# One attention-and-MLP kernel: the first block's second MLP product by quarters of w_ch2, and the scaling of w_ch2 mostly on GpSimd

## The chip, the cores and the metric

One core of a Trainium2 chip. The metric is the device time of one execution in microseconds (us). Engines are named as the profile names them: PE is TensorE's matmuls and PEld its weight loads, DVE is VectorE, ACT is ScalarE, POOL is GpSimd, SP is SyncE, whose queue issues most DMAs. A "q" behind an engine is its sequencer.

## The reference

A pooled attention over 8 batches of 8 heads, 576 rows and head size 64, followed by a residual MLP mixer on 512 channels:

```python
k_p = k.reshape(B, H, Sp, pool, D).mean(axis=3)        # pool = 8, Sp = 72
v_p = v.reshape(B, H, Sp, pool, D).mean(axis=3)
scores = scale * np.matmul(q, k_p.transpose(0, 1, 3, 2))
attn = softmax(scores)
x = np.matmul(attn, v_p)                               # then (B, S, H*D) = (8, 576, 512)

a1 = alpha1 * x + beta1
tok = np.einsum('ts,bsd->btd', w_tok, a1)
u = x + lam * tok
a2 = alpha2 * u + beta2
ch = np.maximum(a2 @ w_ch1, 0.0) @ w_ch2               # 512 -> 2048 -> 512
return u + lam * ch
```

## The kernel before, in words

**Blocks and chunks.** The 8 x 576 rows are cut into 36 chunks of 128 rows, and four chunks make a block; nine blocks (`n` = 0 to 8) go through the MLP one after the other. While block `n` is in the MLP, batch `n + 1` goes through attention, so that PE always has matmuls of one or the other.

**The MLP of a block.** `mlp_A(n, j)` makes one of 16 slices of the hidden layer: four matmuls into a PSUM tile `ps_h` (L662), then a ReLU on ACT into `H4` (L669). `mlp_B(n, m, part)` (L674) is the second product for chunk `m` and one quarter `part` of w_ch2: four matmuls (L682) that add to the chunk's PSUM tile. Behind the last quarter DVE adds the result to the chunk `u_sb` (L689), and `store` issues the output on SP's queue (L698). This plain form is used in blocks 0 and 1 only (`FIRST = 2`). From block 2 on, the second product is a 2 x 2 Strassen-like scheme (`product`, L748) on sums of quarters of w_ch2, which DVE makes once, late in block 1 (`weight_sum`, L712).

**lam.** In block 0 w_ch2 is as loaded, and DVE multiplies the product by `lam_bc` in PSUM (L688) before it adds it (L689). From block 1 on, w_ch2 itself has been multiplied by lam: `scale_w2(g, i)` (L709) does one of the four pieces of quarter `g`, 128 x 512 in bf16, in place (L710). There are 16 pieces. A piece can be scaled only when block 0 has used it for the last time, and must be done before block 1 uses it.

**The order of the work** is written out by hand. In each block a list `todo` of (position, step) is sorted by position, and the steps are issued in that order; every engine then runs its own instructions strictly in that order and waits on semaphores for the others. Position 16 is where the second product of a block starts.

**Attention of the next batch, as far as it is touched.** `load_q_bf` loads q through GpSimd's queue (L79); SP transposes it into `qT` (L397). `sum_k` (L185, L187) sums pairs of k rows on GpSimd, `att_K` makes the pooled k on PE (`ps_kp`, L445 and L451), and DVE copies it to `kp` (L457). `att_V` sums pairs of v rows on DVE in three halvings (L483: 72 x 1024, 72 x 512, 72 x 256). `att_S4` makes the scores from `qT` and `kp` (`ps_s`, L513; `ps_r`, L520), ACT takes the exponentials (L542), and `att_AV` multiplies by v (`ps_av`, L556, L560); DVE normalizes (L562, L564) and scales (`xs`, L578, L571). `mix_T` mixes the tokens (`ps_tok`, L614), DVE adds x (L618), ACT casts (L622), and `mix_uT` has SP transpose the result into `u_fm` for the next block's `mlp_A` (L633).

**PSUM.** Two buffers of tag `ch` hold the products of chunks 0 and 1; six buffers of tag `gp` serve all else, the products of chunks 2 and 3 (`ps_ch2`) included. A new tile waits until the engine that reads the old one is done.

Of the kernel before, what the change touches and what calls it, by code (L numbers as in the profile page):

```python
# [11 lines left out]
ALU = mybir.AluOpType  # L12
# [11 lines left out]
def kernel(  # L24
# [18 lines left out]
    nc = tc.nc  # L43
# [23 lines left out]
    def new_batch(b):  # L67
        st1[b] = {"qT": [None] * 2, "ET": [None] * H, "raw": [None] * 2, "q": [None] * 2,
                  "k": [None] * 2, "v": [None] * 2}
# [130 lines left out]
    lam_bc = const.tile([P, DM], FP, tag="lam_bc", name="lam_bc")  # L200
# [66 lines left out]
    for i in range(2):  # L267
# [11 lines left out]
                            in1=pool_v[0:32, 1:16:2], op=ALU.add)  # L279
# [74 lines left out]
    w2 = [const.tile([P, 4, DM], BF, tag=f"w2_{g}", name=f"w2_{g}") for g in range(4)]  # L354
# [8 lines left out]
    def scale_w1(i, cc):  # L363
        nc.scalar.activation(out=w1[i][:, cc, :], in_=w1[i][:, cc, :], func=AF.Copy, bias=0.0,
                             scale=al2_cols[:, cc:cc + 1])
# [285 lines left out]
    def mlp_A(n, j, t0=0, t1=512):  # L651

        if t0 == 0:
            ps_A[j] = gp("ps_h")
        ps_h = ps_A[j]
        one = t1 < 512
        for cc in range(4):
            if n == 0:
                rhs = u_fm[0][:, cc, 0, 0:257] if one else u_fm[0][:, cc, t0 // 256:2, 0:256]
            else:  # L660
                rhs = u_fm[n][:, cc, :]
            nc.tensor.matmul(out=ps_h[:, t0:t1 + one], lhsT=w1_of(cc, j), rhs=rhs,  # L662
                             start=(cc == 0), stop=(cc == 3))
        if one:
            nc.vector.tensor_copy(out=bias_cols[:, j:j + 1], in_=ps_h[:, 256:257])
            return
        if (n, j // 4) not in H4:
            H4[n, j // 4] = work.tile([P, 4, 512], BF, tag="H4", bufs=4, name="H4")
        nc.scalar.activation(out=H4[n, j // 4][:, j % 4, :], in_=ps_h, func=AF.Relu,  # L669
                             bias=bias_cols[:, j:j + 1], scale=1.0)  # L670
# [3 lines left out]
    def mlp_B(n, m, part):  # L674
        if part == 0:
            if m < 2:
                ps_ch[m] = psB.tile([P, DM], FP, tag="ch", bufs=2, name="ps_ch")
            else:
                ps_ch[m] = gp("ps_ch2")
        ps = ps_ch[m]  # L680
        for j in range(4 * part, 4 * part + 4):
            nc.tensor.matmul(out=ps, lhsT=H_of(n, j)[:, 128 * m:128 * m + 128], rhs=w2[j // 4][:, j % 4, :],  # L682
                             start=(j == 0), stop=(j == NJ - 1))
        if part == 3:
            b, c = chunks[4 * n + m]
            u = st2[b, c]["u"]
            if n == 0:
                nc.vector.tensor_tensor(out=ps, in0=lam_bc, in1=ps, op=ALU.mult)  # L688
            nc.vector.tensor_tensor(out=u, in0=u, in1=ps, op=ALU.add)  # L689
            store(n, m)  # L690
# [15 lines left out]
    HALF = DM // 2  # L706
    wino = {}

    def scale_w2(g, i):  # L709
        nc.vector.tensor_tensor(out=w2[g][:, i], in0=w2[g][:, i], in1=lam_bc, op=ALU.mult)  # L710

    def weight_sum(i, g):  # L712
        lo, hi = w2[g], w2[g + 2]
# [20 lines left out]
    def hidden_sum(n, i, g):  # L734

        lo, hi, S2, S3 = H4[n, g], H4[n, g + 2], wino["S2"][g], wino["S3"][g]
        top, low = slice(0, HALF), slice(HALF, DM)
        o, a, b, op = {
            3: (S3, lo[:, :, top], lo[:, :, low], ALU.subtract),
            1: (lo[:, :, low], lo[:, :, low], hi[:, :, low], ALU.add),  # L740
            2: (S2, lo[:, :, low], lo[:, :, top], ALU.subtract),
            4: (lo[:, :, top], hi[:, :, top], S2, ALU.subtract),
        }[i]
        nc.vector.tensor_tensor(out=o, in0=a, in1=b, op=op)  # L744
# [189 lines left out]
    for n in range(NBLK):  # L934
        todo = []
        for j in range(0 if n else 4, NJ):
            if n == 0 and j < 8:
                todo.append((j, lambda j=j: mlp_A(0, j, 0, 256)))
                todo.append((j + (1.01 if j < 7 else 0.3), lambda j=j: mlp_A(0, j, 256, 512)))
            else:  # L940
                at = 8 * (j // 4 % 2) + 4 * (j // 8) + j % 4 if n >= FIRST else j
                todo.append((at, lambda j=j: mlp_A(n, j)))
        for m in range(4 if n < FIRST else 0):
            for part in range(4):
                at = 16 + 2 * part + (m if m < 2 else 6 + m)
                todo.append((at, lambda m=m, part=part: mlp_B(n, m, part)))
        if n == 0:
            for i in range(3):
                for cc in range(4):
                    todo.append((17.0 + 2.0 * i + 0.5 * cc, lambda i=i, cc=cc: scale_w1(i, cc)))  # L950
            for piece in range(8):
                at = 27.3 + 0.55 * piece
                todo.append((at, lambda k=piece: scale_w2(k // 4, k % 4)))
        if n == FIRST - 1:
            for piece in range(8):
                todo.append((1.0 + 1.7 * piece, lambda k=piece: scale_w2(2 + k // 4, k % 4)))
            for s, i in enumerate((1, 3, 2)):
                for g in range(2):
                    todo.append((23.2 + 2.6 * s + 1.3 * g, lambda i=i, g=g: weight_sum(i, g)))
        if n == FIRST:  # L960
            for g in range(2):
                todo.append((1.2 + g, lambda g=g: weight_sum(4, g)))
        if n >= FIRST:
            last = n == NBLK - 1
            when = ((3, (4.6, 14.6)), (1, (8.6, 19.2)), (2, (8.8, 19.4)), (4, (22.3, 23.0)))
            if last:
                when = ((3, (4.6, 12.6)), (1, (8.6, 16.1)), (2, (8.8, 16.2)), (4, (18.6, 19.6)))
            for i, at in when:
                for g in range(2):
                    todo.append((at[g], lambda i=i, g=g: hidden_sum(n, i, g)))  # L970
            order = (1, 2, 5, 6, 4, 7, 3) if last else (1, 2, 4, 5, 6, 3, 7)
            for s, i in enumerate(order):
                for pp in range(2):
                    todo.append((16 + 2 * s + pp, lambda i=i, pp=pp: product(n, i, pp)))
                for part in range(2 if i == 7 else 1):
                    todo.append((17.05 + 2 * s + (1.9 if i == 1 and not last else 0) + 0.01 * part,
                                 lambda i=i, part=part: gather(n, i, part)))
            if last:
                for m in range(2):
                    todo.append((19.1, lambda m=m: store(n, m, 0, HALF)))  # L980
                    todo.append((28.1, lambda m=m: store(n, 2 + m, queues=(nc.sync, nc.scalar))))
                    todo.append((29.2, lambda m=m: store(
                        n, m, HALF, DM, ((nc.sync, nc.scalar)[m],) * 2)))
            else:
                for m in range(4):
                    todo.append((27.2 if m < 2 else 29.2, lambda m=m: store(n, m)))
        if n == 0:
            todo.append((6.2, lambda: setup_rowsum(4)))
            todo.append((8.3, setup_wtok_odd))
            for g in range(2, 4):  # L990
                todo.append((4 * g - 0.8, lambda g=g: setup_bias(range(4 * g, 4 * g + 4))))
        b = n + 1
        if b < B:
            todo += attention(b)
            if b + 1 < B:
                new_batch(b + 1)
                gate = nc.vector if b == 1 else None
                for u in range(2):
                    at = (15.31 if b == 1 else 21.0) + 0.01 * u
                    todo.append((at, lambda b=b, u=u: load_k(b + 1, u, gate)))  # L1000
                    at = {1: 14.0, 2: 6.5}.get(b, 0.4) + 0.1 * u
                    todo.append((at, lambda b=b, u=u: load_q_bf(
                        b + 1, u, nc.vector if b == 2 else None)))
                    at = 15.35 + 0.01 * u if b == 1 else (6.7 if b == 2 else 3.5) + 4.0 * u
                    todo.append((at, lambda b=b, u=u: load_v(
                        b + 1, u, behind=nc.vector if b < 3 else None)))
                todo.append((15.3 if b == 1 else 20.9, lambda b=b: load_rem(b + 1, behind=gate)))
        for _, do in sorted(todo, key=lambda x: x[0]):
            do()
# [30 lines left out]
```

## Time and profile before

| | |
|---|---|
| three executions | 341.84, 343.35, 344.87 us; median 343.35 us |
| span of the profiled execution, first to last instruction | 339.7 us |
| what lies around the span | not shown; 3.7 us if the profiled execution is as long as the median, 2.1 to 5.2 us by the other two |
| mean granted PE clock | 0.992 |
| ACT, share of the span | 52% |
| HBM traffic over the span | 141 GB/s |
| L662, first product: 128x512 matmuls | x544, 384 ns each |
| L710, `scale_w2` on DVE | x16, 868 ns each, between 64.6 and 90.0 us |
| L578, `xs` on POOL | x12, 1266 ns each |

A row of groups gives a line of the kernel, engine and operation, the tiles it writes and reads, how often, the busy time and the mean duration of one. A matmul's duration is longer than the distance to the next one, since matmuls overlap: 16 matmuls of 128x512 that follow each other without a wait take 3.46 us from the first start to the next start (50.49 to 53.95 us), 0.216 us each.

### The profile page before, as it was taken

Reading aid. Unit: us, or ns where it says so; the run is one execution under the profiler, and the core shown is the slowest. Engines: PE = TensorE matmul, PEld = TensorE weight load, DVE = VectorE, ACT = ScalarE, POOL = GpSimd, SP = SyncE. Lnnn points to the kernel's source line nnn. Section 1 sums busy time; section 2 is a strip of 40 time slices with the busy share of each in tenths; the row PEclk is TensorE's granted clock in tenths of the full one; section 3 lists DMA queues with packets and bytes.
Section 4 is the critical chain, followed back from the end, with each engine's and each line's share of the span. In section 5 each row is a group of like instructions: output and inputs, shape, how many; then the busy total and the mean of one; then the engine's idle time right before and its main releaser. Section 6 shows DMA issues by size and latency. Waiting matters only on the chain.

```text
span 339.7 us, 6491 instructions
## 1 busy us (share of the span) xinstructions
PE 328.1 (97%) x2524; PEld 209.0 (62%) x2524; DVE 237.3 (70%) x486; ACT 175.4 (52%) x322; POOL 94.5 (28%) x110
## 2 busy tenths in 40 slices
PE   8999999979999999999999999999999999999994
PEld 3768754435444567755775576657765766586583
DVE  7672378699779979687868787786778783263263
ACT  3767989247611880279127913583258325704800
POOL 8869352611029002710162026201420200000000
PEclk9999999998999999999999999999999999999998
DMA  8999989951996994399539943896350035003003
GB/s 123 199 212 266 268 152 267 209 132 38 159 242 116 189 168 127 70 212 181 168 69 206 198 141 68 185 188 190 49 148 2 0 53 149 0 2 125 0 31 95
DMA packets 66168, 45.81 MB, mean 135 GB/s; under 512 B 34349, under 2 KB 56501, under 8 KB 66138
## 3 DMA queue, kind: packets, MB, share of 16 engines
q1 hardware_dynamic: 51788, 32.60, 41.8%
q0 software_dynamic: 13824, 12.40, 22.5%
q10 hardware_dynamic: 526, 0.40, 0.5%
q8 instruction: 20, 0.33, 0.4%
q14 instruction: 10, 0.08, 0.1%
HBM read 38.30 MB, written 9.44 MB: 141 GB/s over the span
## 4 chain that ended last, share of the span: by engine, by line
PE 78%; DVE 15%; DMA 4%; issue 2%; POOL 0%; DVEq 0%
PE ps_h L662 30%; PE ps_w L775 21%; PE ps_tok L614 9%; PE ps_ch L682 7%; DMA v_main<-in_v_dram 4%; DVE w L710 4%; PE ps_av L556 2%; DVE u_sb L793 2%; PE ps_s L513 2%; DVE x_tm L564 2%; PE ps_warm L605 1%; DVE xs L578 1%; DVE v_u L483 1%; DVE H L744 1%; PE ps_kp L445 1%
## 5 line engine op out<-in xcount | busy, mean ns | idle before, releaser
L662 PE MATMUL ps_h<-u_fm,w 128*128 128x512 bf16 (+2 forms) x608 | 135.5, 372 | 1.3 <-DVE u_sb L689 1.0
L669 ACT ACTIVATE H<-ps_h,bias_cols 128x512 bf16<-128x512 f32 x144 | 98.1, 688 | 60.2 <-PE ps_h L662 59.2
L662 PEld LDWEIGHTS <-w 128*128 128x128 bf16 x608 | 65.8, 114 | 52.3 <-issue 5.8
L775 PEld LDWEIGHTS <-H 128*128 128x128 bf16 x560 | 53.0, 98 | 13.3 <-DVE H L744 2.6
L622 ACT CAST u_bf<-u_sb 128x512 bf16<-128x512 f32 x32 | 19.8, 618 | 73.2 <-issue 41.5
L775 PE MATMUL ps_w<-w,H 128*128 128x256 bf16 x448 | 53.8, 273 | 0.0
L793 DVE TENSOR_TENSOR u_sb<-u_sb,ps_w 128x512 f32<-128x512 f32 x54 | 36.4, 685 | 21.7 <-PE ps_w L775 21.1
L578 POOL TENSOR_TENSOR xs<-x_tm,lamal_bc 128x512 bf16<-128x512 f32 x12 | 15.1, 1266 | 110.5 <-DVE x_tm L564 110.3
L614 PE MATMUL ps_tok<-xs,wtT 128*128 128x512 bf16 (+3 forms) x200 | 44.9, 380 | 0.0
L618 DVE TENSOR_TENSOR u_sb<-x_tm,ps_tok 128x512 f32<-128x512 f32 (+1 forms) x40 | 27.4, 685 | 13.4 <-PE ps_tok L614 13.3
L564 DVE TENSOR_TENSOR x_tm<-ps_av,rec 128x320 f32<-128x320 f32 x64 | 31.5, 492 | 2.7
L542 ACT ACTIVATE ET<-ps_s 72x512 f16<-72x512 f32 x56 | 32.3, 591 | 0.0
L682 PE MATMUL ps_ch<-w,H 128*128 128x512 bf16 x128 | 30.4, 379 | 0.0
L614 PEld LDWEIGHTS <-wtT 128*128 128x128 bf16 (+3 forms) x200 | 17.4, 100 | 16.0 <-issue 1.1
L562 DVE RECIPROCAL rec<-ps_av 128x5 f32<-128x5 f32 x64 | 12.2, 191 | 17.0 <-PE ps_av L560 16.7
L483 DVE TENSOR_TENSOR v_u<-v_u 72x1024 f32<-72x1024 f32 (+1 forms) x24 | 22.8, 948 | 0.2
L775 PE MATMUL ps_w<-w_t,h_s 128*128 128x256 bf16 x168 | 22.6, 273 | 0.0
L682 PEld LDWEIGHTS <-H 128*128 128x128 bf16 x128 | 11.9, 98 | 13.7 <-issue 0.4
L185 POOL TENSOR_TENSOR k_raw<-k_raw 128x512 f32<-128x512 f32 x14 | 19.2, 1368 | 0.0
L187 POOL TENSOR_TENSOR k_bf<-k_raw 128x512 bf16<-128x512 f32 x14 | 18.8, 1342 | 1.1
L775 PEld LDWEIGHTS <-h_s 128*128 128x128 bf16 x168 | 16.4, 98 | 4.1
L744 DVE TENSOR_TENSOR h_s<-H 128x1024 bf16<-128x1024 bf16 x21 | 14.5, 690 | 6.3 <-ACT H L669 5.8
(148 smaller groups left out, 349.8 us busy)
## 6 DMA issues: line engine op xcount, KB each, us to landing
out_dram<-u_sb SPq DMA_DIRECT2D x30, 256.0 KB
k_raw<-in_k_dram SPq DMA_DIRECT2D x12, 512.0 KB
v_u<-in_v_dram SPq DMA_DIRECT2D x12, 512.0 KB
q_bf<-in_q_dram POOLq DMA_DIRECT2D x16, 256.0 KB, 6.7
w<-in_moe_w_ch_dram POOLq DMA_DIRECT2D x6, 512.0 KB, 14.2
out_dram<-u_sb SPq DMA_DIRECT2D x10, 128.0 KB
w<-in_moe_w_ch_dram POOLq DMA_DIRECT2D x1, 1024.0 KB, 14.2
k_raw<-in_k_dram POOLq DMA_DIRECT2D x2, 512.0 KB, 17.5
```

The source lines that it names most:

```text
L185: eng.tensor_tensor(out=raw[:, :, 0:2], in0=raw[:, :, 0:2], in1=raw[:, :, 2:4], op=ALU.add)
L483: nc.vector.tensor_tensor(out=out, in0=t[:, :, 0:width], in1=t[:, :, width:2 * width], op=ALU.add)
L542: nc.scalar.activation(out=o, in_=i, func=AF.Exp, bias=0.0, scale=0.125)
L564: nc.vector.tensor_tensor(out=x[:, 1 - odd:6 - odd, dd:dd + D], in0=av[:, :, 0:64], in1=rec.unsqueeze(2).to_broadcast((P, 5, D)), op=ALU.mult)
L614: nc.tensor.matmul(out=ps_tok[p0:p1], lhsT=wtT[0:kk, at, P * c:P * c + p1 - p0], rhs=xs_pool[i][0:kk, sc, :], start=(sc == 0), stop=(sc == 4))
L618: nc.vector.tensor_tensor(out=s["u"][p0:p1, :], in0=x[p0:p1, 1 + c if c < 4 else 5 - 5 * i, :], in1=ps_tok[p0:p1, 0:DM], op=ALU.add)
L622: nc.scalar.copy(out=s["u_bf"], in_=s["u"])
L662: nc.tensor.matmul(out=ps_h[:, t0:t1 + one], lhsT=w1_of(cc, j), rhs=rhs, start=(cc == 0), stop=(cc == 3))
L669: nc.scalar.activation(out=H4[n, j // 4][:, j % 4, :], in_=ps_h, func=AF.Relu, bias=bias_cols[:, j:j + 1], scale=1.0)
L682: nc.tensor.matmul(out=ps, lhsT=H_of(n, j)[:, 128 * m:128 * m + 128], rhs=w2[j // 4][:, j % 4, :], start=(j == 0), stop=(j == NJ - 1))
L775: nc.tensor.matmul(out=ps, lhsT=stat(j), rhs=moving(j), stop=(j == 7), start=(first and (pp == 0 or alone) and j == 0), skip_group_check=True)
L793: nc.vector.tensor_tensor(out=o, in0=o, in1=banks[key, "both"], op=ALU.add)
```

## The change

Three things change in the lists of positions, and one in an engine:

- In block 0 the second product goes quarter by quarter: quarter 0 for chunks 0, 1, 2, 3, then quarter 1 for all four, and so on. Before, chunks 0 and 1 went through all four quarters first, then chunks 2 and 3. So each quarter of w_ch2 is used for the last time earlier, and all four chunks end close together, at positions 28 to 31.
- `scale_w2` runs on GpSimd unless told otherwise. The four pieces of quarter 0 and the first of quarter 1 stand in block 0 at positions 19.1 to 19.4 and 23.1; all eight pieces of quarters 2 and 3 stand at the start of block 1, at 0.5 to 1.2.
- Pieces 1 to 3 of quarter 1 stay on VectorE, at 24.7, 25.8 and 26.9 of block 0.

```diff
-    def scale_w2(g, i):
-        nc.vector.tensor_tensor(out=w2[g][:, i], in0=w2[g][:, i], in1=lam_bc, op=ALU.mult)
+    def scale_w2(g, i, eng=nc.gpsimd):
+        eng.tensor_tensor(out=w2[g][:, i], in0=w2[g][:, i], in1=lam_bc, op=ALU.mult)
...
         for m in range(4 if n < FIRST else 0):
             for part in range(4):
-                at = 16 + 2 * part + (m if m < 2 else 6 + m)
+                at = 16 + (4 * part + m if n == 0 else 2 * part + (m if m < 2 else 6 + m))
                 todo.append((at, lambda m=m, part=part: mlp_B(n, m, part)))
...
-            for piece in range(8):
-                at = 27.3 + 0.55 * piece
-                todo.append((at, lambda k=piece: scale_w2(k // 4, k % 4)))
+            for i in range(4):
+                todo.append((19.1 + 0.1 * i, lambda i=i: scale_w2(0, i)))
+            todo.append((23.1, lambda: scale_w2(1, 0)))
+            for i in range(1, 4):
+                todo.append((23.6 + 1.1 * i, lambda i=i: scale_w2(1, i, nc.vector)))
         if n == FIRST - 1:
             for piece in range(8):
-                todo.append((1.0 + 1.7 * piece, lambda k=piece: scale_w2(2 + k // 4, k % 4)))
+                todo.append((0.5 + 0.1 * piece, lambda k=piece: scale_w2(2 + k // 4, k % 4)))
```

What the built program makes of it: on DVE the four pairs L688, L689 of block 0 now stand in a row behind all five `mix_T` additions (L618); before, two pairs stood before them and two after. On SP the stores of chunks 0 and 1 stood ahead of the transposes into `u_fm`; now chunk 0's stands behind the fourth of these and ahead of the fifth and of the two `qT` transposes, and the other three behind `qT`. On POOL the eight pieces of block 1 stand behind both `sum_k` of batch 2 and ahead of the loads of q for batch 3. On PE the matmuls are the same and as many; in block 0 the token mixing keeps its places in the row of matmuls. In block 1 the `ps_h` tile of j = 4 waits for L689 of chunk 2 (as before), that of j = 5 for L689 of chunk 3 (before, `ps_kp` waited for it), and that of j = 8 for the copy L457 of the second `ps_kp` (before, for an exponential).

## The prediction

> **What bounds the kernel now.** The page first: PE is busy nearly throughout, so only stretches where PE waits, or runs at a lower clock, can be won.
>
> ```profile
> span 339.7 us, 6491 instructions
> PE 328.1 (97%) x2524; PEld 209.0 (62%) x2524; DVE 237.3 (70%) x486; ACT 175.4 (52%) x322; POOL 94.5 (28%) x110
> ```
>
> Next the chain of waits, which has 3.7% (12.6 us) on L710. In order of time (start, length, what) it lies on DVE from 63.15 us to 87.9 us:
>
> ```profile
> 64.57 6.08 DVE w L710 x5
> 70.68 0.70 DVE ps_ch L688
> ...
> 72.01 1.28 DVE w L710 x2
> ...
> 74.54 0.69 DVE w L710
> 75.23 1.13 DVE v_u L483
> ```
>
> PE's timeline in this stretch (start, length, work, in brackets the wait before it) shows what that costs:
>
> ```profile
> 67.53 3.62 PE L662 MATMUL ps_h<-u_fm,w 128*128 128x512 bf16 x16
> 72.14 1.02 PE L662 MATMUL ps_h<-u_fm,w 128*128 128x512 bf16 x4 [0.99 <-DVE u_sb L689]
> 74.68 0.28 PE L445 MATMUL ps_kp<-pool_main,k_bf 128*128 128x64 bf16 x4 [1.51 <-DVE u_sb L689]
> ...
> 74.84 3.57 PE L662 MATMUL ps_h<-u_fm,w 128*128 128x512 bf16 x8
> ...
> 79.04 0.30 PE L513 MATMUL ps_s<-qT,kp 64*72 64x256 bf16 x2 [0.47 <-DVE kp L457]
> ```
>
> Eight matmuls that take 1.73 us elsewhere take 3.4 us from 74.84. The stretches of equal length (busy time of PE, PEld, DVE, ACT, POOL, then the granted clock) say why: half clock, behind a stretch in which PE was busy 1.21 us of 3.42.
>
> ```profile
> 71.44:74.86 3.42, 1.21 (x11) 0.62 (x11) 3.39 (x6) 1.12 (x2) 0.00 (x0) 1.00 0.27 88
> 74.86:78.27 3.41, 3.41 (x15) 1.18 (x12) 3.38 (x6) 0.69 (x1) 0.00 (x0) 0.50 0.23 82
> ```
>
> DVE has next to no idle time from 64.57 to 79.04, so the slow clock cost nothing: the scores L513 had to wait for DVE's copy L457 anyhow.
>
> **What is to be won at most.** In block 1 the first product, with the attention between, lasts from 67.53 to the first L682 at 90.09: 22.56 us. The same work in block 2, in the chain of waits, lasts from 109.01 to 125.45: 16.44 us. So at most 6.1 us are lost here; later blocks are not touched.
>
> **What bounds the new order: DVE and POOL take turns.** When a DVE operation with two inputs in SBUF meets one of POOL, each waits for the other's whole instruction. DVE's L578 at 51.93 took 1.24 us against 0.69 alone, beside POOL's L578 of 51.35 to 52.62. Of the five L710 from 64.57 the first three, beside POOL's `sum_k`, took 1.52, 1.75 and 1.75 us, the other two 0.68; POOL's operations then took 1.72 and 1.60 instead of 1.26:
>
> ```profile
> 64.27 1.26 POOL L187 TENSOR_TENSOR k_bf<-k_raw 128x512 bf16<-128x512 f32 x1
> 65.49 1.72 POOL L185 TENSOR_TENSOR k_raw<-k_raw 128x512 f32<-128x512 f32 x1
> 67.29 1.60 POOL L187 TENSOR_TENSOR k_bf<-k_raw 128x512 bf16<-128x512 f32 x1
> ```
>
> They take turns: POOL 1.2, DVE 0.6. With one input in PSUM DVE does not wait: L618 at 63.15 took 0.69 each beside L185, and L564 its usual 0.49 at 46.70.
>
> **The parts, step by step** (times on the clock of the profile before).
>
> *GpSimd's pieces.* No L710 on POOL is shown. POOL's 128x512 operations take 1.26 to 1.28 us, f32 or bf16 out; I take 1.25 start to start. Bounds: 0.72 (128x256, L173) and 1.72. In block 0 the five pieces start behind POOL's L571 (53.49) and end at about 59.8. POOL was idle until 61.89, and DVE does only L618 meanwhile: cost nothing. If that cover went, `sum_k` and `kp` would come later, with 4 us to spare.
>
> *VectorE's three pieces.* The first, at about 59.8, and the second, at 61.75, lie in waits of DVE for PE (0.94, 1.25 and 1.40 us before L618). The second holds POOL's cast L170 back by about 0.45, so `sum_k` ends at about 68.95 instead of 68.89. The third comes behind L618 at 64.54, meets L185 and ends at about 65.2 (between 65.15 and 66.3).
>
> *Four pairs L688, L689.* One pair takes 1.33 (70.68 to 72.01), with an input in PSUM, so POOL does not matter. Two pairs leave 54.2 to 57.6, where DVE had time, and stand on the path now: four from 65.2 to 70.5. PE's last quarter ends at 64.9 for chunk 0 and 67.5 for chunk 3, so DVE never waits for it. In exchange five pieces in 6.08 us go, and 1.28 + 0.6 x 3 us of further pieces before the copy L457 at 78.54. PE needs the third pair's buffer at 71.0 (done 69.2) and the fourth's at 72.0 (done 70.5): both waits, 0.99 and 1.51, go.
>
> *What is late next.* PE reaches the scores at 67.53 + 28 x 0.216 + 2 x 0.16 = 73.9. They need `kp`, whose copy stands on DVE behind three v sums L483 (1.14 + 0.60 + 0.34 start to start). All have two SBUF inputs, and POOL's eight pieces run from 68.95. Turn by turn: DVE is ready at 70.5, POOL's second piece ends at 71.45, sum to 72.6; piece to 73.85, sum to 74.45; piece to 75.7, sum to 76.05; copy 0.45, no turn: 76.45. **PE waits 2.6 us.** The scores take 0.72 and j = 7 0.87, until 78.1; j = 8 waits for the second copy: piece to 77.3, sum 1.15 to 78.45, copy to 78.85. **0.8 us.** The normalization of the heads costs about 0.2 more. POOL ends at about 83.15. The second product starts at 67.53 + 16.44 + 3.6 = 87.6 instead of 90.09: **2.5 us gained.** DVE's first turn can come up to 0.95 earlier or 0.3 later, and its third piece end 1.1 later: 1.4 to 3.5.
>
> *SP's queue.* The store of chunk 0 waits for L689 at 66.55; behind it are a transpose for block 2 and the two for `qT`. Transposes take 1.2 to 1.3 each, a store 0.4: the first `qT` is issued by 69.6 and the second by 70.9, against 69.0 and 70.4 before. A `u_fm` transpose issued until 66.10 was in use at 67.53. Needed at 76.5: cost nothing, and under 1 us were the DVE wait gone. The other stores move from 55.7 into time when DMA is idle.
>
> **The rivals.** *The sums of v do not wait for POOL.* L483 is never beside POOL in this trace (72 partitions, f32). Then the copy is done at 73.1, PE never waits: 6.1 us gained, 337.2 us. Against it: L578 is f32 too, and waited. [...]
>
> *The clock.* A wait of 2.6 us can be followed by half clock, as 2.2 us of idle time in one stretch was; whether depends on where the stretches of 3.41 us begin. It costs 3.41 x 0.5 = 1.7, of which 0.8 falls into the second wait: 1.6 gained, 341.8 us. [...]
>
> *Given back at block 2.* q for batch 3 is loaded behind POOL's last piece, at 83.15 instead of 82.01, and SP's transposes of it hold up loads and the `u_fm` transposes: 1.1 later, ending their issue by 105.0 where block 2 would start at 106.35. The 1.35 left is what sufficed at 67.53. DMA is busy there: up to 2.5 given back, 343.4 us.
>
> *Slower: POOL gives no turn.* If its eight ready pieces follow each other without a turn for DVE, the sums start at 68.95 + 8 x 1.25 = 78.95 and the copy is done at 81.5 instead of 78.99: 2.5 lost, and a wait of 7.6 us brings half clock, 1 to 1.7 more: 347.2 us. It decides from a copy later than 79.0, that is from more than one lost turn of 1.25 per sum. Against it: at 65.49 and 67.29 POOL did wait its turn.
>
> **How the numbers follow.** The profiled span is 339.7, and 343.35 is the median of runs from 341.84 to 344.87; I take the gain from the median. The forecast, 2.5 gained, 340.8 us, has 0.42; clock 0.18; free sums 0.18; given back 0.10; no turn 0.12. The range 337.0 to 343.8 takes in the first four but for their outer ends, with half a spread of the runs on either side. One per cent, 3.4 us, is about what a measurement here can tell from no change. Faster by more: the free sums and about a quarter of the forecast, 0.28; slower: no turn, 0.11; the rest 0.61.
>
> **What would show it.** Right: 13 L710 on POOL at 1.25, more beside DVE; no PE wait on L689; a PE wait of 1.6 to 2.9 us on L457 before L513, with L483 at 1.5 to 2.4 us; then one of under 1 us before j = 8. L483 at 1.21 would make it the first rival. Wrong altogether, if PE waits in block 0, or if the shift at the second product of block 1 is not found at the end of the span.

## The result, and the profile after

| | before | after |
|---|---|---|
| median | 343.35 us (15 runs, 341.38 to 345.96) | 339.49 us (15 runs, 337.73 to 342.57) |
| after / before | | 0.9903, 95% interval 0.9876 to 0.9929 |
| profiled execution, span | 339.7 us | 340.4 us (the execution took 342.39 us) |

The change gained 3.9 us between the medians, and 3.3 us (2.4 to 4.3) by the ratio; 2.5 were forecast, with 340.8 us as the time and 337.0 to 343.8 as the range. By the ratio, one per cent is just not reached.

The profiled execution after has the longer span, although its kernel is the faster one. First the page of after, then PE's timeline (start, length, work, the wait before it in brackets). A few records of matmuls are missing from the traces: PE issues the same matmuls as before, though the page counts x2493 in place of x2524.

```profile
span 340.4 us, 6464 instructions
PE 328.5 (97%) x2493; PEld 211.4 (62%) x2524; DVE 230.9 (68%) x473; ACT 176.0 (52%) x322; POOL 112.4 (33%) x123
```

```profile
70.81 4.48 PE L662 MATMUL ps_h<-u_fm,w 128*128 128x512 bf16 x20
...
79.04 0.30 PE L513 MATMUL ps_s<-qT,kp 64*72 64x256 bf16 x2 [1.68 <-DVE kp L457]
...
79.75 4.47 PE L662 MATMUL ps_h<-u_fm,w 128*128 128x512 bf16 x11
...
90.70 1.03 PE L682 MATMUL ps_ch<-w,H 128*128 128x512 bf16 x4
```

Block 1 begins at 70.81 instead of 67.53, and its first product, with the attention between (from here on "the stretch"), ends at the first L682, at 90.70: 19.89 us instead of 22.56. Both waits on L689 are gone, and one of 1.68 us before the scores is left. DVE and POOL in the same time:

```profile
74.06 3.26 DVE L483 TENSOR_TENSOR v_u<-v_u 72x1024 f32<-72x1024 f32 x2
77.35 1.26 DVE L483 TENSOR_TENSOR vp<-v_u 72x256 f16<-72x256 f32 x1
78.54 0.44 DVE L457 CAST kp<-ps_kp 128x288 bf16<-128x288 f32 x1
```

```profile
57.18 5.65 POOL L710 TENSOR_TENSOR w<-w,lam_bc 128x512 bf16<-128x512 bf16 x5
...
72.37 12.24 POOL L710 TENSOR_TENSOR w<-w,lam_bc 128x512 bf16<-128x512 bf16 x8
84.56 1.55 POOL L79 DMA_DIRECT2D q_bf<-in_q_dram  x2
```

The five pieces of block 0 took 1.13 us each; the eight of block 1 took 1.5 each, since they and the v sums took turns: the three L483 before the first copy lasted 1.68, 1.54 and 1.26 us, where they last 1.21, 0.68 and 0.42 with POOL idle.

**What the spans say.** In every profile of this study, the time from the end of the stretch to the end of the span is 249.6 to 249.8 us. So a span is the start of block 1, plus the stretch, plus 249.6:

| profile | block 1 starts | stretch | span |
|---|---|---|---|
| before | 67.53 | 22.55 | 339.7 |
| before, second profile (`before_again`) | 71.76 | 23.51 | 344.9 |
| after | 70.81 | 19.88 | 340.4 |
| after, second (`after_again`) | 67.38 | 18.69 | 335.6 |
| after, third (`after_again2`) | 67.27 | 18.69 | 335.6 |
| `order_only` | 68.07 | 24.96 | 342.6 |
| `engines_only` | 69.98 | 23.20 | 343.0 |
| `no_late` | 68.69 | 16.44 | 334.7 |
| `act_copies` | 69.39 | 18.34 | 337.3 |
| `late_behind_q` | 67.57 | 25.59 | 342.8 |
| `gap_op` | 67.14 | 23.89 | 340.7 |
| `late_gated` | 67.39 | 23.93 | 340.9 |
| `no_meeting` | 83.00 | 16.44 | 349.1 |
| `apart` | 70.06 | 16.44 | 336.1 |

The start moves by over 4 us between two executions of one kernel. That is settled early: the first L614 stands at 21.01 and 25.52 in the two profiles of before. Of after, the windows from 10.00 to 18.70 us (busy time and instructions of PE, PEld, DVE, ACT, POOL) show PE busy nearly throughout in both, with 79 matmuls in the first profile and 109 in the second:

```profile
10.00:18.70 8.70, 8.70 (x79) 6.73 (x77) 4.88 (x14) 4.38 (x13) 4.34 (x6) 1.00 1.23 205
```

```profile
10.00:18.70 8.70, 8.50 (x109) 6.08 (x109) 7.00 (x21) 6.74 (x20) 6.36 (x8) 1.00 1.23 208
```

The same matmuls are slower there in the first profile: eight L402 take 1.01 us from 16.43, and 0.61 us from 13.81 in the second. The trace's record of the granted clock begins at 18.73 us in the first and at 10.00 in the second (the windows show 1.00 where there is no record). In the first profile of before it begins at 10.00, and eight L402 take 1.03 us from 6.27 and 0.61 from 13.49. All profiles agree with this: the first L614 stands at 21.0 to 21.8 us in the eight whose record begins at 8.9 to 10.4, at 22.7 where it begins at 14.2, and at 23.4 to 25.5 in the four where it begins at 16.8 to 19.7; `act_copies`, with a record from 8.7 and the first L614 at 23.3, has half clock from 18.9 to 22.4. So the start moves with the time at which PE comes to full clock, and not with the change.

So single spans are compared below by their stretches, and whole kernels by their ratios.

### The profile page after: what moved, and what is told of

Read it like the earlier page. It is cut to its first block, busy times and chain, and to the rows that moved or that the text cites. A ratio compares the mean times of both kernels' runs of the same rounds, so it can differ in the third digit from the quotient of the medians.

```text
span 340.4 us, 6464 instructions
## 1 busy us (share of the span) xinstructions
PE 328.5 (97%) x2493; PEld 211.4 (62%) x2524; DVE 230.9 (68%) x473; ACT 176.0 (52%) x322; POOL 112.4 (33%) x123
## 4 chain that ended last, share of the span: by engine, by line
PE 86%; DVE 8%; DMA 2%; issue 2%; POOL 0%; DVEq 0%; POOLq 0%
PE ps_h L662 36%; PE ps_w L775 21%; PE ps_tok L614 9%; PE ps_ch L682 8%; PE ps_s L513 2%; PE ps_av L556 2%; DVE u_sb L793 2%; DMA q_bf<-in_q_dram 2%; DVE x_tm L564 1%; DVE xs L578 1%; DVE v_u L483 1%; PE ps_kp L445 1%; DVE H L744 1%; PE ps_sc L493 1%; PE ps_q L402 1%
## 5 line engine op out<-in xcount | busy, mean ns | idle before, releaser
L662 PE MATMUL ps_h<-u_fm,w 128*128 128x512 bf16 (+2 forms) x588 | 134.3, 371 | 1.3 <-DVE bias_cols L665 0.2
L662 PEld LDWEIGHTS <-w 128*128 128x128 bf16 x608 | 65.8, 114 | 51.3 <-issue 4.6
L578 POOL TENSOR_TENSOR xs<-x_tm,lamal_bc 128x512 bf16<-128x512 f32 x12 | 15.2, 1267 | 109.2 <-DVE x_tm L564 109.0
L614 PE MATMUL ps_tok<-xs,wtT 128*128 128x512 bf16 (+2 forms) x193 | 44.5, 380 | 0.4
L618 DVE TENSOR_TENSOR u_sb<-x_tm,ps_tok 128x512 f32<-128x512 f32 (+1 forms) x40 | 27.4, 684 | 15.2 <-PE ps_tok L614 15.1
L682 PE MATMUL ps_ch<-w,H 128*128 128x512 bf16 x124 | 30.0, 379 | 0.2
L614 PEld LDWEIGHTS <-wtT 128*128 128x128 bf16 (+3 forms) x200 | 17.4, 100 | 16.0 <-issue 1.1
L562 DVE RECIPROCAL rec<-ps_av 128x5 f32<-128x5 f32 x64 | 12.2, 191 | 20.0 <-PE ps_av L560 19.7
L483 DVE TENSOR_TENSOR v_u<-v_u 72x1024 f32<-72x1024 f32 (+1 forms) x24 | 25.0, 1040 | 0.2
L682 PEld LDWEIGHTS <-H 128*128 128x128 bf16 x128 | 11.9, 98 | 13.7 <-issue 0.4
L187 POOL TENSOR_TENSOR k_bf<-k_raw 128x512 bf16<-128x512 f32 x14 | 18.9, 1353 | 1.1
L185 POOL TENSOR_TENSOR k_raw<-k_raw 128x512 f32<-128x512 f32 x14 | 18.7, 1335 | 0.0
```

Source lines behind the costliest of these rows:

```text
L187: eng.tensor_tensor(out=bf, in0=twice[0], in1=twice[1], op=ALU.add)
L483: nc.vector.tensor_tensor(out=out, in0=t[:, :, 0:width], in1=t[:, :, width:2 * width], op=ALU.add)
L614: nc.tensor.matmul(out=ps_tok[p0:p1], lhsT=wtT[0:kk, at, P * c:P * c + p1 - p0], rhs=xs_pool[i][0:kk, sc, :], start=(sc == 0), stop=(sc == 4))
L618: nc.vector.tensor_tensor(out=s["u"][p0:p1, :], in0=x[p0:p1, 1 + c if c < 4 else 5 - 5 * i, :], in1=ps_tok[p0:p1, 0:DM], op=ALU.add)
```

## The experiments

Ratios are to the kernel before, run beside it on the same chip.

**`order_only` and `engines_only`: the parts alone.** The first has the new order with all sixteen pieces on VectorE at the old positions:

```diff
-                todo.append((19.1 + 0.1 * i, lambda i=i: scale_w2(0, i)))
+                todo.append((27.3 + 0.55 * i, lambda i=i: scale_w2(0, i, nc.vector)))
...
-                todo.append((0.5 + 0.1 * piece, lambda k=piece: scale_w2(2 + k // 4, k % 4)))
+                todo.append((1.0 + 1.7 * piece, lambda k=piece: scale_w2(2 + k // 4, k % 4, nc.vector)))
```

> Quarter by quarter order kept, but all 16 pieces on VectorE at the positions of the kernel before. If the gain needs the move to GpSimd: VectorE has eight pieces and four pairs L688, L689 in a row behind the mixing; by the rows of before the copy L457 comes about 2 us later than before (about 81 us on the clock of the profile before), PE waits for L689 and for L457 again, and the kernel is 1 to 3 us slower than before (ratio 1.003 to 1.009). If the order alone brought the gain: ratio 0.99.

The second has the old order, with the pieces of block 0 at the old positions and thirteen of the sixteen on GpSimd:

```diff
-                at = 16 + (4 * part + m if n == 0 else 2 * part + (m if m < 2 else 6 + m))
+                at = 16 + 2 * part + (m if m < 2 else 6 + m)
...
```

> Old order (chunks 0 and 1 first, then 2 and 3), 13 pieces on GpSimd and three on VectorE. Quarter 0 is then free only behind its last use, late in block 0, so that five pieces stand between GpSimd's cast and sum_k. If the two parts need each other: sum_k ends 6 to 7.5 us later, PE waits on POOL's L187 or on L457, and the kernel is 1.5 to 4 us slower than before (ratio 1.004 to 1.012). If taking work off VectorE was enough: ratio 0.99 or less.

Measured: 1.0085 (1.0051 to 1.0119) and 1.0039 (1.0007 to 1.0071), the latter just below its range. Each part alone is a little slower, and both together are faster. PE's timeline of `order_only`, then of `engines_only`:

```profile
74.28 1.89 PE L662 MATMUL ps_h<-u_fm,w 128*128 128x512 bf16 x8 [1.56 <-DVE u_sb L689]
...
81.17 0.43 PE L513 MATMUL ps_s<-qT,kp 64*72 64x256 bf16 x2 [4.85 <-DVE kp L457]
```

```profile
77.01 0.29 PE L445 MATMUL ps_kp<-pool_main,k_bf 128*128 128x64 bf16 x4 [0.64 <-POOL k_bf L187]
...
81.31 0.30 PE L513 MATMUL ps_s<-qT,kp 64*72 64x256 bf16 x2 [3.98 <-DVE kp L457]
```

The order alone puts four pairs L688, L689 ahead of the copies and leaves DVE the pieces. The engines alone put POOL's early pieces ahead of `sum_k`, because the old order frees quarter 0 too late for POOL's idle time. The order is what makes that idle time usable.

**`no_late`: what the eight late pieces cost.** They are left out, so quarters 2 and 3 of w_ch2 stay unscaled from block 1 on.

```diff
-                todo.append((0.5 + 0.1 * piece, lambda k=piece: scale_w2(2 + k // 4, k % 4)))
+                pass
```

> The kernel after, with quarters 2 and 3 of w_ch2 left unscaled (the eight GpSimd pieces of block 1 left out). If turns between GpSimd's pieces and VectorE's v sums make the remaining wait: the three kinds of L483 take 1.21, 0.68 and 0.42 us again, PE's wait before the scores L513 goes (under 0.3 us), no half clock follows, and the stretch from the first L662 of block 1 to its first L682 falls from 19.9 to about 16.6 us; ratio to before 0.980 to 0.984. If something else holds L457 (late v, late qT, the pairs L688 and L689 alone): the wait of 1 to 2 us stays, ratio 0.99.

Measured: 0.982 (0.9787 to 0.9852).

```profile
71.96 1.93 DVE L483 TENSOR_TENSOR v_u<-v_u 72x1024 f32<-72x1024 f32 x2
73.93 0.42 DVE L483 TENSOR_TENSOR vp<-v_u 72x256 f16<-72x256 f32 x1
```

The sums run free, PE waits nowhere (L513 stands at 75.16, 6.47 behind the start, with no wait), and the stretch is 16.44 us, as block 2's in the profile before. So all that after still lost, 2.25 to 3.44 us of stretch, came from these eight pieces.

**`act_copies`: the copies out of the queue.** The two copies L457 of batch 2 go to ScalarE.

```diff
-                         lambda u=u: att_K(b, u, nc.vector.tensor_copy)))
+                         lambda u=u: att_K(b, u, nc.scalar.copy if b == 2 else nc.vector.tensor_copy)))
```

> The kernel after, with the two copies L457 of batch 2 on ScalarE instead of VectorE. If only the place of the copy behind the v sums on VectorE holds the scores: the v sums stay long (1.2 to 2.2 us each) but PE's wait before L513 goes; some 0.6 us is then lost at the normalization, and the stretch falls from 19.9 to 17.2 to 18.2 us; ratio to before 0.983 to 0.987. If the turns bind through v itself: PE waits at L556 instead, ratio 0.99.

Measured: 0.9876 (0.9839 to 0.9913), a smaller gain than the first case had, and PE now waits at L556, as the second had it.

```profile
75.86 0.30 PE L513 MATMUL ps_s<-qT,kp 64*72 64x256 bf16 x2
...
82.93 0.29 PE L556 MATMUL ps_av<-vp,ET 72*128 72x66 f16 x4 [0.52 <-DVE x_tm L564]
...
83.56 1.05 PE L662 MATMUL ps_h<-u_fm,w 128*128 128x512 bf16 x4 [0.30 <-DVE x_tm L564]
```

The wait before the scores is gone. The v sums still took turns until 82.10 (the second three in 2.18, 1.36 and 1.27 us), now the normalization behind them was late, and PE waited there three times (a last wait of 0.21 stands before the next L513): the stretch is 18.34 us. A wait moved along a queue and kept most of its size.

**`after_again`, `after_again2`, `before_again`: the same kernels again.**

> The changed kernel once more, unaltered, for a second profile and a second ratio. If the start-up of TensorE makes the difference between the spans of the first two profiles (340.4 after, 339.7 before), this profile's span goes with the time at which its first L662 of block 1 starts, and the stretch from there to the first L682 of block 1 is 18.2 to 19.9 us: 19.9 with TensorE at half clock behind its wait before L513, 18.2 to 18.6 without. If the change gained only by chance of the first chip, the ratio is above 0.995; otherwise 0.987 to 0.993.

> The changed kernel a third time, for one more profile: the wait before L513 again 1.5 to 2.7 us, and half clock behind it or not, as the phase of the windows of 3.41 us falls; a stretch of 18.2 to 19.9 us.

> The kernel before once more, unaltered, for a second profile. Theory of the turns: the stretch from the first L662 of block 1 to its first L682 is the same 22.6 us within 0.5, since its waits come from VectorE's eight L710 between the v sums. If the stretch depends on the phase of the clock instead, it differs by over 1 us.

Measured for `after_again`: 0.9882 (0.9818 to 0.9945), median 338.90 us. The ratio is as expected, and the stretch, 18.69, just above the 18.2 to 18.6 expected without half clock. The other two are single executions. PE's timeline of `after_again`:

```profile
67.38 4.48 PE L662 MATMUL ps_h<-u_fm,w 128*128 128x512 bf16 x20
...
75.61 0.30 PE L513 MATMUL ps_s<-qT,kp 64*72 64x256 bf16 x2 [1.69 <-DVE kp L457]
...
77.71 1.89 PE L662 MATMUL ps_h<-u_fm,w 128*128 128x512 bf16 x8 [0.33 <-DVE v_u L158]
...
86.07 1.03 PE L682 MATMUL ps_ch<-w,H 128*128 128x512 bf16 x4
```

The second wait, 0.33, is the one before j = 8; its bracket names L158, which DVE does next behind the second copy L457. The wait before the scores is the same to 0.01 us, but here full clock follows it. The windows, cut in the steps of 3.41 us in which the record of the clock runs (in the first profile 61.44 us full, 3.41 half, 256.00 full: 18, 1 and 75 steps; PE's busy time first, the granted clock third from the end), of the first profile of after, of `after_again` and of `after_again2`:

```profile
76.76:80.17 3.41, 1.72 (x22) 1.12 (x21) 3.38 (x4) 1.41 (x5) 3.41 (x4) 1.00 0.37 130
80.17:83.59 3.42, 3.34 (x8) 1.18 (x8) 3.25 (x8) 2.20 (x5) 3.42 (x3) 0.50 0.08 8
```

```profile
71.44:74.85 3.41, 2.48 (x22) 1.38 (x20) 3.34 (x3) 2.34 (x4) 3.41 (x2) 1.00 0.95 286
74.85:78.27 3.42, 2.28 (x18) 1.39 (x20) 3.29 (x9) 1.76 (x5) 3.42 (x3) 1.00 0.02 8
```

```profile
73.87:77.28 3.41, 1.72 (x15) 1.04 (x17) 3.41 (x4) 1.44 (x4) 3.41 (x3) 1.00 0.16 58
77.28:80.70 3.42, 3.10 (x23) 1.76 (x23) 3.15 (x10) 3.21 (x6) 3.42 (x3) 1.00 0.33 89
```

In the first profile the wait fell into one window, with PE busy for 1.72 us of 3.41. In the second it was split over two, busy for 2.48 and 2.28. In the third it fell into one window again, also with 1.72. Half clock followed only in the first. So the phase alone does not settle it: behind 1.72 of 3.41 us busy both came, and what decides there is open. Half clock cost 1.69 us (twelve L662, of which eleven have records, in 4.47 us instead of 2.78) and hid the wait of 0.33, so that the stretch grew by 1.19. Both profiles of before have half clock too: twelve L662 in 4.47 us in the second, eight in 3.57 in the first. The second's stretch, 23.51, lies 0.96 from the first, between what the two theories had expected. So this loss can befall both kernels.

**`late_behind_q`: the late pieces behind the loads of q.**

```diff
-                todo.append((0.5 + 0.1 * piece, lambda k=piece: scale_w2(2 + k // 4, k % 4)))
+                todo.append((6.75 + 0.1 * piece, lambda k=piece: scale_w2(2 + k // 4, k % 4)))
```

> The changed kernel with its eight late pieces of w_ch2 issued on GpSimd behind the two q loads of block 1 (position 6.75 in place of 0.5), everything computed. With those eight pieces left out the time was 0.982 of the kernel before and the stretch from the first L662 of block 1 to its first L682 took 16.45 us, against 19.89 with them. Theory of the turns: what the pieces cost is only that they stand beside VectorE's v sums and, through TensorE's wait, its clock; behind the q loads they run from about 78 to 88 us, beside normalizations that read PSUM, and two scalings L578 that wait a turn each: a stretch of 16.5 to 17.3 us and a ratio of 0.982 to 0.986. Rival, given back at block 2: the pieces now end some 4 to 5 us later and GpSimd's L578 of heads 4 and 5 and the q loads' neighbours come late; the second product would wait on w before L682, and the ratio would stay at 0.988 to 0.993. [...]

Measured: 1.0094 (1.0059 to 1.0128), with a stretch of 25.59 us. Both the theory (16.5 to 17.3 us) and the rival "given back at block 2" (0.988 to 0.993) fall, and the loss lies in one place. POOL's timeline, DVE's, and PE's:

```profile
75.40 1.55 POOL L79 DMA_DIRECT2D q_bf<-in_q_dram  x2 [6.21 <-DVE v_u L158]
76.96 8.97 POOL L710 TENSOR_TENSOR w<-w,lam_bc 128x512 bf16<-128x512 bf16 x8
```

```profile
76.02 10.20 DVE L483 TENSOR_TENSOR vp<-v_u 72x256 f16<-72x256 f32 x1
```

```profile
86.97 0.40 PE L556 MATMUL ps_av<-vp,ET 72*128 72x66 f16 x4 [6.37 <-DVE x_tm L564]
```

A sum of 0.42 us stood for 10.20 us, until the last of eight pieces was done. POOL's pieces took 1.12 each, as if DVE had asked for nothing. This is the rival "POOL gives no turn" of the prediction, met in the same block by the same instructions, with the train some 8 us later than in after (9.4 us behind the start of block 1 instead of 1.6).

**`gap_op` and `late_gated`: why no turn?** Both keep that place. The first puts a small POOL operation between the loads and the pieces, the second a POOL copy that waits for the last v sum:

```diff
...
+            todo.append((6.65, lambda: nc.gpsimd.memset(probe, 0.0)))
             for piece in range(8):
-                todo.append((0.5 + 0.1 * piece, lambda k=piece: scale_w2(2 + k // 4, k % 4)))
+                todo.append((6.75 + 0.1 * piece, lambda k=piece: scale_w2(2 + k // 4, k % 4)))
```

> The version with the eight late pieces behind the two q loads, and between loads and pieces one GpSimd memset of 128x1. Without it VectorE's last v sum (72x256, f16) stood for 10.20 us, from 76.02, while GpSimd's second q load was being issued, until the last of the eight pieces ended: no turn at all, and a ratio of 1.0094. Theory A, the load: a VectorE operation that meets GpSimd while it issues a load, with a piece queued next, has lost its turn for the whole train; an operation in between ends that, and the last v sum takes 0.4 to 2 us: ratio 0.982 to 0.988. Theory B, who asked first: VectorE asked before the train began and GpSimd serves what was queued when it asked; the memset changes nothing, the sum again takes 9 to 11 us: ratio 1.006 to 1.013.

```diff
...
+            todo.append((8.05, lambda: nc.gpsimd.tensor_copy(
+                out=probe[0:SPG], in_=vp1_pool[1][:, 0, 0:1])))
             for piece in range(8):
-                todo.append((0.5 + 0.1 * piece, lambda k=piece: scale_w2(2 + k // 4, k % 4)))
+                todo.append((8.06 + 0.01 * piece, lambda k=piece: scale_w2(2 + k // 4, k % 4)))
```

> The same, with a GpSimd copy of 72x1 that reads the last v sum in the place of the memset, so that the eight pieces begin when all v sums are done, at about 76.5 to 78 us. VectorE's next operations with two SBUF inputs are L578 and L571 of the two pairs of heads, some 3 to 6 us later, in the middle of the train. If turns are given in the middle of a train, as in the changed kernel (L483 1.26 to 1.80 us), L578 takes 1.2 to 1.8 instead of 0.69, the stretch from the first L662 of block 1 to its first L682 is 16.5 to 17.5 us, and the ratio is 0.982 to 0.987. If this place gives none, L578 stands until the train's end (87 us), 5 to 7 us, and the ratio is 1.000 to 1.010.

Measured: 1.0048 (1.0011 to 1.0085) and 1.0032 (1.0005 to 1.0059). DVE's timeline of `gap_op`, then of `late_gated`:

```profile
75.58 0.42 DVE L483 TENSOR_TENSOR vp<-v_u 72x256 f16<-72x256 f32 x1
...
78.76 7.34 DVE L578 TENSOR_TENSOR xs<-x_tm,lamal_bc 128x512 bf16<-128x512 f32 x1
```

```profile
79.00 7.44 DVE L578 TENSOR_TENSOR xs<-x_tm,lamal_bc 128x512 bf16<-128x512 f32 x1
```

The last v sum ran free in both. In `gap_op` it stood, as in `late_behind_q`, about 1 us ahead of the first piece, so an operation between load and piece did matter to it: that part of theory A held. The rest of A fell, and B with it: in the middle of the train, with no load in front of the pieces, the next operation with two SBUF inputs got no turn either, for the 6 pieces still to come. For `late_gated` its second case came true. What decides between turns and none is not settled. In four kernels (after, `act_copies`, `engines_only`, and before with other operations) each request was served after at most one piece; in three none was. The form of the waiting operation alone is not it: the same `vp` sum took 1.26 in after and 10.20 in `late_behind_q`. But the L578 of `gap_op` and `late_gated` is another form than the sums, and no run shows an L578 served inside a train of pieces: in `engines_only` one asked during the last piece, took 1.64 us and ended 0.55 us behind the train. So for these two the form stays a rival, though the L578 of 1.24 us in before waited for one POOL operation only. The three trains without a turn stand behind the loads of q, and the trains with turns behind `sum_k`; whether that is the cause was not tried apart from the place.

**`no_meeting`: the pieces spread.**

```diff
-            for i in range(4):
-                todo.append((19.1 + 0.1 * i, lambda i=i: scale_w2(0, i)))
-            todo.append((23.1, lambda: scale_w2(1, 0)))
+            for i in range(3):
+                todo.append((4.0 + 0.1 * i, lambda i=i: scale_w2(0, i)))
+            for pc in range(3, 8):
+                todo.append((19.1 + 0.1 * pc, lambda pc=pc: scale_w2(pc // 4, pc % 4)))
             for i in range(1, 4):
-                todo.append((23.6 + 1.1 * i, lambda i=i: scale_w2(1, i, nc.vector)))
+                todo.append((23.6 + 1.1 * i, lambda i=i: scale_w2(2, i - 1, nc.vector)))
...
-            for piece in range(8):
-                todo.append((0.5 + 0.1 * piece, lambda k=piece: scale_w2(2 + k // 4, k % 4)))
+            for pc in range(11, 16):
+                at = 8.05 if pc < 13 else 12.65
+                todo.append((at, lambda pc=pc: scale_w2(pc // 4, pc % 4, nc.vector)))
```

> The changed kernel with the pieces spread anew so that no piece of GpSimd stands beside VectorE's v sums: three pieces of quarter 0 on GpSimd in its idle time of block 0 (42.8 to 46.3 us, once w_ch2's first quarter has landed), five in the place where the change has five, VectorE's three as they are, and of the last five two on VectorE behind the last v sum of block 1 (idle there for 1.27 us in the run without the late pieces) and three behind its last normalization of the second half (idle for 2.3 us). Theory of the turns: the late pieces cost nothing but their meeting with the v sums, so this computes everything at the time of the run without them: L483 at 1.21, 0.68 and 0.42 us, no wait before L513, a stretch from the first L662 of block 1 to its first L682 of 16.4 to 16.9 us, a ratio of 0.981 to 0.985. Rival, the work itself costs wherever it stands: VectorE's five pieces of 0.6 us come onto the path (L564 late, the wait before j = 12 or before L682 grows): a stretch of 17.5 to 19.5 us and a ratio of 0.986 to 0.991.

Measured: 1.0315 (1.0265 to 1.0365). Ten pieces now stand ahead of all or part of block 0's reading of them. So block 0's second product waits for pieces, and in parts of quarters 0 to 2 it carries lam twice: not everything is computed as in the changed kernel. PE's timeline:

```profile
56.15 0.59 PE L682 MATMUL ps_ch<-w,H 128*128 128x512 bf16 x1 [4.50 <-POOL w L710]
...
79.12 4.04 PE L682 MATMUL ps_ch<-w,H 128*128 128x512 bf16 x17 [2.73 <-DVE w L710]
```

With three more waits on POOL (0.53 each) and two more on DVE (1.38 and 1.18), PE waited 11.4 us in block 0, and its clock was half from 54.1 to 64.4 us. The whole time therefore says nothing on the theory, but the stretch does: with five late pieces on VectorE it was 16.44 us, as without any.

**`apart`: block 0 as in the change, the late pieces where nothing meets.**

```diff
-            for piece in range(8):
-                todo.append((0.5 + 0.1 * piece, lambda k=piece: scale_w2(2 + k // 4, k % 4)))
+            todo.append((0.5, lambda: scale_w2(2, 0)))
+            for pc in range(9, 16):
+                at = 8.05 if pc < 12 else 12.65
+                todo.append((at, lambda pc=pc: scale_w2(pc // 4, pc % 4, nc.vector)))
```

> The changed kernel with its block 0 as it is and the eight late pieces set where no operation of GpSimd with tiles in SBUF meets one of VectorE with two: one on GpSimd behind the k sums (it ends before the first v sum starts), three on VectorE behind the last v sum, four behind the second L571. Everything is computed as in the changed kernel. In the run with five late pieces on VectorE the stretch from the first L662 of block 1 to its first L682 took 16.44 us, as without any late piece. Theory: the late pieces cost only where they meet the v sums or a normalization; so a stretch of 16.4 to 16.8 us, L483 at 1.21, 0.68 and 0.42 us, and a ratio of 0.980 to 0.985, faster than the changed kernel (0.988 to 0.990) by 0.5 to 0.9 per cent. Rival: VectorE's seven pieces of 0.6 us make L562 and L564 late (0.3 us behind the first three, 0.1 behind the four) and with them the buffers that TensorE waits for: a stretch of 17 to 18 us and a ratio of 0.985 to 0.989.

Measured: 335.56 us, ratio 0.976 (0.971 to 0.981), a little below the expected range and faster than both kernels. DVE's timeline:

```profile
73.31 1.94 DVE L483 TENSOR_TENSOR v_u<-v_u 72x1024 f32<-72x1024 f32 x2
...
78.85 1.89 DVE L710 TENSOR_TENSOR w<-w,lam_bc 128x512 bf16<-128x512 bf16 x3
...
85.32 2.48 DVE L710 TENSOR_TENSOR w<-w,lam_bc 128x512 bf16<-128x512 bf16 x4
```

The seven pieces fill gaps of DVE at 0.6 us each, the sums run free, and the stretch is 16.44 us: its whole loss is gone. The ratio is a little below what the stretch explains: 0.982 with the first profile of before (6.1 of 343 us), 0.979 with the second (7.1 us), of which the interval holds the latter. That remainder was not followed.

## Why the prediction came out as it did

- **Turns between DVE and POOL**: shown. L483 took 1.68, 1.54 and 1.26 us, where the forecast had 1.5 to 2.4; without the late pieces it took 1.21, 0.68 and 0.42. That each waits for the other's whole instruction agrees with these rows, but not with `late_behind_q`: there a sum of 0.42 us stood for 10.20, until eight instructions of POOL were done.
- **The size of the wait**: this is the term that was off. Forecast were 2.6 us before the scores, 0.8 before j = 8 and 0.2 at the normalization, 3.6 in all. Against the 16.44 us of `no_late` and `apart`, `after_again` lost 2.25: the scores came 1.76 us later (8.23 us behind the start of block 1 instead of 6.47), 0.49 went before j = 8, and nothing at the normalization. What was too long is a turn of one piece and one sum: from the end of one sum to the end of the next it took 1.58 and 1.29 us, where the forecast has 1.85 and 1.60. Pieces were reckoned at 1.25 and took 1.13 where nothing met them. With the first sum 0.13 early, the first copy ended 8.18 us behind the start of block 1 instead of 8.92.
- **The clock**, a rival at 0.18, came in the first profile and not in the two others. It brought the loss of that profile back to 3.44 us, near the forecast of 3.6. That this profile's gain, 22.55 less 19.88, is 2.67 us and so near to 2.5 is luck: two errors cancel. Where the stretches of 3.41 us begin did not alone settle whether it came: behind 1.72 us busy came half clock in the first profile and full clock in the third.
- **L689, stores, `sum_k`, block 0**: as forecast. PE waits on no L689 and nowhere in block 0, and VectorE's three pieces cost it nothing; the four pairs end 0.3 us later than forecast, against the start of block 1.
- **Given back at block 2**: refuted, by 249.6 to 249.8 us behind the stretch in all profiles.
- **Free v sums**: refuted for the change, and its price confirmed by `no_late`: 22.55 less 16.44 is the 6.1 us that it gave.
- **POOL gives no turn**: not in the change. The argument against it, that POOL had waited its turn elsewhere in the trace, held there and failed in `late_behind_q`. It was evidence from one place, not a rule.

The mechanism was right, and its price 1.35 us too high where the clock stays full: 22.55 less 18.69 is 3.86 us gained, beside 2.5 in the forecast, 3.3 by the ratio and 3.9 between the medians. That 3.86 and 3.9 agree so closely is partly chance: the stretch differs by about 1 us between profiles of one kernel, with half clock or without.

## What to carry to other kernels

Work moved to an idle engine was free here only while it stood beside no operation with which it took turns: the five pieces of block 0 cost PE no wait, the eight beside the v sums 2.25 to 3.44 us of stretch. So look for which operations of the other engine stand beside it, piece by piece. A place with turns in one trace does not promise turns at another place (the same `vp` sum took 1.26 us in after and 10.20 in `late_behind_q`); keep a long train of GpSimd operations away from a VectorE operation with two SBUF inputs that something waits for, as `apart` does (16.44 us of stretch, 2.25 less than `after_again`). When one execution moves by several us at its start, compare the stretch that the change touches, not the spans.

## What the runs showed of the hardware that had not been expected

- A train of GpSimd pieces can hold a VectorE operation with two SBUF inputs to the train's end (10.20 us for a sum of 0.42, 7.34 and 7.44 for an L578 of 0.69), or let it through behind one piece (1.68, 1.54 and 1.26 us in after for sums of 1.21, 0.68 and 0.42). What decides which of the two is open.
- In the first profiles of before and after, half clock followed windows of 3.41 us in which PE was busy for 1.21 us (71.44 to 74.86, before), 0.86 us (334.27 to 337.68, before) and 1.72 us (76.76 to 80.17, after), and the empty one at the end of after; full clock followed all others within the record, the least busy with 2.63 us (85.10 to 88.51, before). In `after_again` it followed 2.28 and 2.48 us, and in `after_again2` 1.72 us, so that at 1.72 us both came. One early window of `act_copies` does not fit: half clock came behind 3.08 us busy (15.52 to 18.94).
- The record of full clock begins anywhere from 8.7 to 19.7 us into the span. Between 10.0 and 18.7 us PE got through 79 matmuls in one execution and 109 in another, and the whole kernel ends that much later. It moves the start of block 1 between 67.1 and 71.8 us, more than the change gains.
